# One body for each extra item in nested conditionals, and the item table ahead of the first weight splits

## The chip, the core and the metric

The kernel runs on one core of one Trainium2 chip. The metric is the device time of one execution in microseconds (us); a kernel is timed in several runs and the median counts. Five engines work side by side, each through its own queue: TensorE (PE in the profile, with its weight loads as PEld), VectorE (DVE), ScalarE (ACT), GpSimd (POOL), and SyncE (SP), which only issues transfers. A name with a q behind it (PEldq, SPq, DVEq) is the sequencer of that engine, which reads the instructions, evaluates branches and passes the work on.

## The reference, cut to what matters

```python
attn_out = _attn_ref(q, k, v)                # 8 x 8 heads, 576 rows of 64; keys and values pooled by 8
x = attn_out.transpose(0, 2, 1, 3).reshape(4608, 512)
# experts: 8 of them, each token goes to the one with the largest logit
expert_idx = np.argmax(logits, axis=1)
for e in range(8):
    mask = expert_idx == e
    h = np.maximum(x[mask] @ w1[e], 0.0)     # 512 -> 1024
    out[mask] = gate_w[mask, None] * (h @ w2[e])   # 1024 -> 512
# feed forward
h = out @ w_in                               # 512 -> 2048
return ((h * np.cos(h)) @ w_out)             # 2048 -> 512
```

All arrays are float32. How many tokens go to an expert is only known when the kernel has computed the logits.

## The kernel before

The kernel has three stages: attention with routing (to about 220 us of the profile), the experts (to about 762 us), and the feed-forward part (to the end). The instructions of an engine stand in its queue in the order in which the code issues them; nothing is reordered.

**Items.** Attention writes each token's row to a buffer `xv` in memory, sorted by expert, through indirect transfers that GpSimd issues (`scatter`). `tables` then computes on VectorE, from the number of tokens of each expert, a table with one row for each *item*: an item is up to 128 tokens of one expert. `tab` holds the row of `xv`, the half of the weight buffer and the expert of each item, `cumi` the running number of items, `crow` the output row. There are at least 36 items (`NTILE`, 4608/128) and at most 43 (`NI`); with this input 41 are computed. The first 36 are a plain loop. How many more there are is read from `cumi` into a register (`more`) on TensorE, VectorE and SyncE.

**One item i.** `gemm1(i)` reads from `tab` which weights to use (two register loads on TensorE), waits until they are there (`sem_ready1`), does 24 matmuls into two banks and VectorE applies the relu into `h`. `load(i+3)` fetches a later item's rows on SyncE's queue, `t_x(i+1)` transposes the next item's rows on TensorE (4 transposes) and VectorE splits them in two float32r parts, `gemm2(i-1)` does the second matrix for the item before (24 matmuls), VectorE scales the result and SyncE stores it (L719 to L724), and `t_h` transposes `h` (8 transposes) and VectorE splits it (4 instructions). So TensorE's order is gemm1(i), t_x(i+1), gemm2(i-1), t_h, gemm1(i+1) and so on.

**Weights.** Every weight matrix is used as a high and a low part. A matrix comes in four chunks of 128x1024 into one of 8 raw buffers; `w_hi` rounds a chunk on ScalarE (L129), `w_lo` subtracts the rounded from the raw one (L137) on GpSimd or VectorE. Chunks 0 to 3 are the first matrix of expert 0, chunks 4 to 7 the first matrix of expert 1, 8 to 11 the second matrix of expert 0, 12 to 15 the second of expert 1. With the last chunk of a matrix `sem_ready1` or `sem_ready2` is raised, on which gemm1 or gemm2 waits. The raw buffers of chunks 0 to 7 are filled during attention; chunk j + 8 is loaded when chunk j has been split. Later chunks are all split on GpSimd, by `phase_x`.

**The start of the expert stage** (L896 to L912) is issued in this order: `tables` on VectorE; the loads of items 0 to 2 on SyncE; chunks 3, 6, 7 on GpSimd; chunks 0, 1, 2, 4, 5 on VectorE behind the table; the loads of chunks 8 to 14; `t_x(0)`.

**The end of the loop.** `either` is a binary tree of conditionals with a copy of the remaining items in each of its eight leaves (`items(k)` with k = 0 to 7, so 28 bodies). With 41 items the program goes to `items(5)`. ScalarE and GpSimd take no part in the conditionals. After them come the transposes `t_y` of the first output rows for the feed-forward part, `gemm2` of the last item with the gate that was copied to `gl`, and the feed-forward loop.

Of the kernel before, what the change touches and what calls it, by code (L numbers as in the profile page):

```python
# [18 lines left out]
ENGINES = mybir.EngineType.PE, mybir.EngineType.DVE, mybir.EngineType.SP  # L19
# [3 lines left out]
def attention_moe_ffn_kernel(  # L23
# [13 lines left out]
    nc = tc.nc  # L37
# [4 lines left out]
    E = w1.shape[0]  # L42
# [5 lines left out]
    NTILE = NT // 128  # L48
    REG = NT + 128
    XW = DM + 2  # L50
    NI = NTILE + E - 1
# [17 lines left out]
    def bank(i, name):  # L69
        return psp[0].tile([128, 512], F32, tag=f"p{i}", name=name)  # L70
# [26 lines left out]
    cumi = const.tile([128, E], I32, name="cumi")  # L97

    sem_ready1 = tc.alloc_semaphore("w1_ready")
    sem_ready2 = tc.alloc_semaphore("w2_ready")  # L100
    sem_w1 = tc.alloc_semaphore("items_past_w1")
    sem_free = tc.alloc_semaphore("items_done")


    raws = {}
# [29 lines left out]
    def w_lo(j, eng):  # L135
        t, hi, lo = raws.pop(j)
        i = eng.tensor_tensor(lo, t, hi.bitcast(F32), ALU.subtract)  # L137
        if eng is nc.gpsimd:
            tc.add_to_no_dep_group(W_GROUP, i.ins)
        c = order[j][1]  # L140
        if c % 4 == 3:
            nc.gpsimd.engine_nop().then_inc(sem_ready2 if c > 3 else sem_ready1, 1)

    def apart(group, dma):

# [445 lines left out]
    def tables(sm):  # L591
        V = nc.vector
        cnt, m, ends, ge, g2, top = (sm.tile([128, E], F32, name=t) for t in ("cnt", "m", "ends", "ge", "g2", "top"))
        mi = sm.tile([128, E], I32, name="mi")
        ii, of, ei = (sm.tile([128, 1], F32, name=t) for t in ("ii", "of", "ei"))
        V.tensor_tensor(cnt, base, ebase, ALU.subtract)
        V.tensor_scalar(mi, cnt, 127.0, None, op0=ALU.add)
        V.tensor_scalar(mi, mi, 7, None, op0=ALU.logical_shift_right)
        V.tensor_scalar(m, mi, 1.0, None, op0=ALU.max)
        V.tensor_tensor_scan(ends, one8, m, 0.0, op0=ALU.mult, op1=ALU.add)  # L600
        V.tensor_scalar(ii, ends[:, E - 1:E], -1.0, iot, op0=ALU.add, op1=ALU.min)
        V.tensor_scalar(ge, ends, ii, None, op0=ALU.is_le)
        V.tensor_copy(cumi, ends)
        V.tensor_reduce(ei, ge, axis=AX.X, op=ALU.add)
        V.tensor_tensor(g2, ge, m, ALU.mult)
        V.tensor_scalar(tab[:, 2:3], ei, 1.0, None, op0=ALU.add)
        V.tensor_reduce(of, g2, axis=AX.X, op=ALU.add)
        V.tensor_scalar(tab[:, 1:2], tab[:, 2:3], 1, None, op0=ALU.bitwise_and)
        V.tensor_scalar(of, of, ii, -128.0, op0=ALU.subtract, op1=ALU.mult)

        V.tensor_scalar(top, cnt, -128.0, 0.0, op0=ALU.add, op1=ALU.max)
        V.tensor_scalar(g2, idx8[:, 0, :], NEG, ei, op0=ALU.subtract, op1=ALU.is_equal)
        V.tensor_tensor(g2, g2, top, ALU.mult)
        V.tensor_reduce(ii, g2, axis=AX.X, op=ALU.add)
        V.tensor_tensor(of, of, ii, ALU.min)
        V.tensor_scalar(tab[:, 1:2], tab[:, 1:2], float(SLOT), None, op0=ALU.mult)
        V.scalar_tensor_tensor(tab[:, 0:1], ei, float(REG), of, op0=ALU.mult, op1=ALU.add)
        V.tensor_tensor(g2, ge, cnt, ALU.mult)
        V.tensor_reduce(ei, g2, axis=AX.X, op=ALU.add)
        V.tensor_tensor(crow, ei, of, ALU.add)  # L620
# [14 lines left out]
    def experts_and_feed_forward(slot, wes):  # L635
# [26 lines left out]
        def split(p, hi, lo):  # L662
            pv = p.rearrange("p (k n) -> p k n", k=4)
            nc.vector.tensor_copy(hi, pv)
            nc.vector.tensor_tensor(lo, pv, hi.bitcast(F32), ALU.subtract)

        def t_x(i):
            t = X[i][:, 0:DM].rearrange("p (c k) -> p k c", k=KC)
            p = bank(0, "ptx")
            for kk in range(KC):  # L670
                nc.tensor.transpose(p[:, kk * 128:(kk + 1) * 128], t[:, kk, :], ident)
            split(p, *xT)
# [26 lines left out]
        def t_h():  # L699
            hv = h.rearrange("p (c k) -> p k c", k=FC1)  # L700
            for n in range(FC1 // 4):
                p = bank(4 + n, "pth")
                for kk in range(4):
                    nc.tensor.transpose(p[:, kk * 128:(kk + 1) * 128], hv[:, n * 4 + kk, :], ident)
                split(p, *hT[n])
# [20 lines left out]
        def gate(i):  # L726
            return X[i][:, DM:XW]
# [53 lines left out]
        def wc_load(f):  # L781
            if f < FC2:
                wraw[f] = rawp[0].tile([128, QW], F32, tag="raw", name="wst")
                if f < 3:
                    d = nc.scalar.dma_start(wraw[f], wd[:, f])
                    d.then_inc(sem_wc[f], 16)
                    tc.no_tile_sem_insts.add(d.ins.name)
                    tc.add_to_no_dep_group(f"wc_load{f}", d.ins)
                else:
                    nc.sync.dma_start(wraw[f], wd[:, f])  # L790
# [16 lines left out]
        def y_load(g):  # L807
            for r in range(4):
                n = g * 4 + r
                Y[n] = (xp.tile([128, XW], F32, tag="x", name="yb") if g else y0p.tile([128, XW], F32, tag=f"y{r}", name="yb"))[:, 0:DM + 1]  # L810
                nc.sync.dma_start(Y[n], yv[n * 128:(n + 1) * 128, :])

        def t_y(g, r, b):
            if r == 0:
                X2[g] = x2p[g % 2].tile([128, 2, KC, 512], F32R, tag="x2", name="x2")
            n = g * 4 + r
            t, x2 = Y.pop(n), X2[g][:, :, :, r * 128:(r + 1) * 128]
            p = bank(b, "pt2")
            for kk in range(KC):
                nc.tensor.transpose(p[:, kk * 128:(kk + 1) * 128], t[:, 0:DM].rearrange("p (c k) -> p k c", k=KC)[:, kk, :], ident)  # L820
            pv = p.rearrange("p (k n) -> p k n", k=KC)

            def rest():
                nc.vector.tensor_copy(x2[:, 0], pv)
                nc.vector.tensor_tensor(x2[:, 1], pv, x2[:, 0].bitcast(F32), ALU.subtract)
                nc.vector.tensor_copy(POS[:, n:n + 1], t[:, DM:DM + 1])

            return rest
# [65 lines left out]
        for n in range(NTILE - CHUNKS[-1], NTILE):  # L894
            scatter(n)
        tables(const)  # L896
        for i in range(3):
            load(i)
        for j in (3, 6, 7):
            w_lo(j, nc.gpsimd)  # L900
        for j in (0, 1, 2, 4, 5):
            w_lo(j, nc.vector)
        for j in range(NB, 2 * NB - 1):
            if j == NB + 4:
                conv_load(0)
# [7 lines left out]
        prev = None  # L913
        for i in range(NTILE):
            ex = gemm1(i)
            load(i + 3)
            t_x(i + 1)
            if i:
                gemm2(i - 1, prev, gate(i - 1))
            t_h()  # L920
            prev = ex
            if i == 0:
                phase_x(slot, 16, 8 * E)
            conv_to(i - 1)
            if i == NTILE - 3:
                ces.close()
                y0p = pool("y0p", 1, bes)
            if i == NTILE - 2:
                y_load(0)

        X[NTILE + 3] = xp.tile([128, XW], F32, tag="x", name="xb")
        for i in range(NTILE + 4, NI):
            X[i] = X[i - 5]
        gl, gl2 = (const.tile([128, 2], F32, name=t) for t in ("gl", "gl2"))
        more = nc.values_load(cumi[0:1, E - 1:E], engines=ENGINES, min_val=NTILE, max_val=NI)

        def items(k):
            ex = prev
            for i in range(NTILE, NTILE + k):
                new = gemm1(i)  # L940
                if i + 3 < NTILE + k:
                    load(i + 3)
                if i + 1 < NTILE + k:
                    t_x(i + 1)
                gemm2(i - 1, ex, gate(i - 1))
                t_h()
                ex = new
            nc.vector.tensor_copy(gl, gate(NTILE + k - 1))

        def either(k0, k1):  # L950
            if k1 - k0 == 1:
                items(k0)
                return
            with tc.If(more < NTILE + (k0 + k1) // 2) as cmp:
                either(k0, (k0 + k1) // 2)
            with cmp.Else():
                either((k0 + k1) // 2, k1)

        either(0, E)
        wes.close()  # L960
        x2p = [pool("x2a", 1, side="right")]
        cp = pool("cp", 2, side="right")
        cn = pool("cn", 1, side="right")
        for f in range(3):
            wc_load(f)

        nc.scalar.activation(gl2, gl, AF.Copy)
        for f in range(3):
            wc_split(f, False, W_GROUP)
        for fn in [t_y(0, r, r) for r in range(4)]:  # L970
            fn()
        gemm2(NI, expert(NI), gl)
        bes.close()
        x2p.append(pool("x2b", 1))
# [3 lines left out]
        for n in range(NS + 2):  # L978
# [5 lines left out]
            rest = None  # L984
            if n < NS:
                g, f = seq[n]
                ff1(n)
                if g + 1 < NG:
                    if f == 3:
                        y_load(g + 1)  # L990
                    if f in (6, 8, 10, 12):
                        rest = t_y(g + 1, (f - 6) // 2, 7)
# [21 lines left out]
NB = 8  # L1014
# [41 lines left out]
```

## Time and profile before

| | us |
|---|---|
| median of 3 runs | 1590.6 |
| lowest, highest | 1588.93, 1591.7 |
| the profiled execution | 1594.11 |
| its span, first to last instruction | 1592.4 |
| TensorE busy | 1514.1 (95%) |
| VectorE busy | 1067.1 (67%) |
| ScalarE busy | 413.8 (26%) |
| GpSimd busy | 348.3 (22%) |
| mean granted TensorE clock | 0.987 |

The span is what the trace covers; the execution's own time is 1.7 us longer. Busy time counts the instructions of an engine; a branch, a register load or a wait is not in it. A granted clock of 1.0 is 2.4 GHz and 0.5 is 1.2 GHz.

### The profile page before, as it was taken

Reading aid. Unit: us, or ns where it says so; the run is one execution under the profiler, and the core shown is the slowest. Engines: PE = TensorE matmul, PEld = TensorE weight load, DVE = VectorE, ACT = ScalarE, POOL = GpSimd, SP = SyncE. Lnnn points to the kernel's source line nnn. Section 1 sums busy time; section 2 is a strip of 40 time slices with the busy share of each in tenths; the row PEclk is TensorE's granted clock in tenths of the full one; section 3 lists DMA queues with packets and bytes.
Section 4 is the critical chain, followed back from the end, with each engine's and each line's share of the span. In section 5 each row is a group of like instructions: output and inputs, shape, how many; then the busy total and the mean of one; then the engine's idle time right before and its main releaser. Section 6 shows DMA issues by size and latency. Waiting matters only on the chain.

```text
span 1592.4 us, 22377 instructions
## 1 busy us (share of the span) xinstructions
PE 1514.1 (95%) x7700; PEld 1262.0 (79%) x7700; DVE 1067.1 (67%) x1914; ACT 413.8 (26%) x681; POOL 348.3 (22%) x308
## 2 busy tenths in 40 slices
PE   5999939999999999989999999999999999999997
PEld 4888838887888888868778888888888888888885
DVE  4577776888888888835887556656565655656553
ACT  4677633034000000000433222222222222222221
POOL 6456568089000013000442000010101001010100
PEclk9999969999999999989999999999999999999999
DMA  9853358389433334310322001010101001010000
GB/s 325 254 176 130 126 189 303 118 275 326 131 100 106 118 119 143 93 43 28 114 79 67 0 12 42 7 47 8 47 1 47 7 8 47 7 47 0 28 0 27
DMA packets 66947, 149.05 MB, mean 94 GB/s; under 512 B 10248, under 2 KB 26632, under 8 KB 66832
## 3 DMA queue, kind: packets, MB, share of 16 engines
q1 hardware_dynamic: 52272, 97.10, 19.3%
q10 hardware_dynamic: 8800, 31.48, 6.0%
q0 software_dynamic: 5760, 18.92, 3.1%
q8 instruction: 75, 1.23, 0.3%
q14 instruction: 40, 0.33, 0.1%
HBM read 107.29 MB, written 40.17 MB: 93 GB/s over the span
## 4 chain that ended last, share of the span: by engine, by line
issue 38%; PE 12%; POOL 2%; DVE 0%; ACT 0%; POOLq 0%; ACTq 0%
PE ph L839 6%; PE po L865 5%; POOL out_dram L876 2%; PE pt L820 0%; PE py L715 0%; DVE gl L855 0%; DVE gh L854 0%; ACT L852 0%; POOLq L875 0%; DVE u L853 0%; ACT u L849 0%; ACT u L852 0%; ACT o L873 0%; POOLq L876 0%; POOLq L1051 0%
## 5 line engine op out<-in xcount | busy, mean ns | idle before, releaser
L839 PE MATMUL ph<-x,slot 128*128 128x512 f32 x1728 | 426.6, 396 | 0.0
L839 PEld LDWEIGHTS ph<-x,slot 128*128 128x128 f32 x1728 | 324.5, 188 | 77.0
L865 PE MATMUL po<-slot,gh 128*128 128x512 f32 x1152 | 382.4, 393 | 0.0
L865 PEld LDWEIGHTS po<-slot,gh 128*128 128x128 f32 x1152 | 216.8, 188 | 47.2
L865 PE MATMUL po<-slot,gl 128*128 128x512 f32 x576 | 226.1, 393 | 0.9 <-DVE gl L855 0.9
L137 POOL TENSOR_TENSOR slot<-raw,slot 128x1024 fp32r<-128x1024 f32 x59 | 139.8, 2403 | 258.9 <-ACT slot L129 258.7
L692 PE MATMUL ph<-slot,xh 128*128 (+1 forms) x656 | 178.3, 404 | 17.4 <-issue 7.5
L876 POOL DMA_INDIRECT out_dram<-o,POS x36 | 37.8, 1049 | 694.3 <-ACT o L873 686.1
L849 ACT ACTIVATE u<-ph,quarter 128x512 f32<-128x512 f32 x144 | 98.9, 686 | 348.8 <-PE ph L839 347.9
L850 DVE TENSOR_SCALAR nr<-u 128x512 f32<-128x512 f32 x144 | 62.2, 432 | 164.4 <-ACT u L849 164.4
L853 DVE TENSOR_TENSOR u<-u,ph 128x512 f32<-128x512 f32 x144 | 99.1, 688 | 100.6 <-ACT u L852 100.6
L692 PEld LDWEIGHTS ph<-slot,xh 128*128 128x128 f32 x656 | 121.9, 191 | 44.8 <-issue 7.7
L129 ACT ACTIVATE slot<-raw 128x1024 fp32r<-128x1024 f32 x64 | 66.5, 1060 | 332.6 <-DVEq L696 241.6
L852 ACT ACTIVATE u<-u 128x512 f32<-128x512 f32 x144 | 91.0, 632 | 219.3 <-DVE u L851 217.8
L865 PEld LDWEIGHTS po<-slot,gl 128*128 128x128 f32 x576 | 108.3, 188 | 24.7 <-DVE gl L855 2.2
L855 DVE TENSOR_TENSOR gl<-u,gh 128x512 fp32r<-128x512 f32 x144 | 112.3, 780 | 4.9
L851 DVE TENSOR_TENSOR u<-u,nr 128x512 f32<-128x512 f32 x144 | 99.8, 693 | 5.0
L715 PE MATMUL py<-slot,h0h 128*128 (+1 forms) x328 | 92.0, 402 | 0.0
L692 PE MATMUL ph<-slot,xl 128*128 (+1 forms) x328 | 91.2, 400 | 0.0
L715 PE MATMUL py<-slot,h1h 128*128 (+1 forms) x328 | 88.1, 390 | 0.0
L854 DVE CAST gh<-u 128x512 fp32r<-128x512 f32 x144 | 76.0, 528 | 14.5 <-DVE u L853 0.5
L800 POOL TENSOR_TENSOR slot<-wst,slot 128x512 fp32r<-128x512 f32 x32 | 43.0, 1367 | 192.1 <-ACT slot L796 192.1
(170 smaller groups left out, 1863.4 us busy)
## 6 DMA issues: line engine op xcount, KB each, us to landing
raw<-in_moe_w_dram ACTq DMA_DIRECT2D x57, 512.0 KB, 5.8
xb<-xv SPq DMA_DIRECT2D x41, 257.0 KB, 3.2
yv<-y SPq DMA_DIRECT2D x41, 256.5 KB, 3.2
yb<-yv SPq DMA_DIRECT2D x36, 256.5 KB, 3.6
kraw<-in_k_dram SPq DMA_DIRECT2D x12, 768.0 KB, 8.6
vraw<-in_v_dram SPq DMA_DIRECT2D x12, 768.0 KB, 9.9
q<-in_q_dram SPq DMA_DIRECT2D x8, 1024.0 KB, 10.2
craw<-in_moe_w_in_dram SPq DMA_DIRECT2D x16, 512.0 KB, 4.5
```

The costliest lines, as they stand in the source:

```text
L137: i = eng.tensor_tensor(lo, t, hi.bitcast(F32), ALU.subtract)
L692: mm = nc.tensor.matmul(p, a[:, kk, :], at(so, o + kk * F1 + n * 512), start=(c == 0), stop=(c == 3 * KC - 1))
L715: mm = nc.tensor.matmul(p, a[:, kk, :], at(so, o + W2O + (n * 4 + kk) * DM), start=(c == 0), stop=(c == 3 * FC1 - 1))
L839: nc.tensor.matmul(p, win[:, f, s, kk * 128:(kk + 1) * 128], x2[:, m, kk, :], start=(c == 0), stop=(c == 3 * KC - 1))
L849: nc.scalar.activation(u, p, AF.Identity, scale=1.0 / TWO_PI_EXACT, bias=quarter)
L851: nc.vector.tensor_tensor(u, u, nr, ALU.subtract)
L852: nc.scalar.activation(u, u, AF.Sin, scale=TWO_PI)
L853: nc.vector.tensor_tensor(u, u, p, ALU.mult)
L854: nc.vector.tensor_copy(gh, u)
L855: nc.vector.tensor_tensor(gl, u, gh.bitcast(F32), ALU.subtract)
L865: nc.tensor.matmul(O[g][r], a[:, r * 128:(r + 1) * 128], wout[:, f, s, :], start=(f == 0 and c == 0), stop=(f == FC2 - 1 and c == 2))
L876: apart("out_rows", nc.gpsimd.indirect_dma_start(out=out, out_offset=bass.IndirectOffsetOnAxis(ap=POS[:, g * 4 + r:g * 4 + r + 1], axis=0) ...
```

## The change

The binary tree of conditionals goes; in its place stands a chain of seven conditionals, each nested in the one before, with one body each. The register `more` is read two items earlier. `t_h` of the 36th item leaves the loop and becomes the first step of the first conditional; each body begins with the `t_h` of the item before it, and one `t_h` follows behind the whole chain. A body prepares the next item whether there is one or not (`load`, `t_x`). The gate of the last item is copied to `gl` ahead of the chain and again in each body.

At the start of the expert stage VectorE takes chunks 0 to 3 and GpSimd chunks 4 to 7. VectorE raises a new semaphore `sem_tab` when it is through with the table and its four chunks, and GpSimd waits for that before its first chunk. `sem_ready1` for expert 0 is raised by VectorE. The transposes `t_y` are issued ahead of the splits `wc_split` (other engines).

```diff
-            nc.gpsimd.engine_nop().then_inc(sem_ready2 if c > 3 else sem_ready1, 1)
+            (nc.gpsimd.engine_nop() if eng is nc.gpsimd else eng.drain()).then_inc(sem_ready2 if c > 3 else sem_ready1, 1)
...
         tables(const)
+        for j in range(4):
+            w_lo(j, nc.vector)
+
+        nc.vector.drain().then_inc(sem_tab, 1)
+        nc.gpsimd.wait_ge(sem_tab, 1)
         for i in range(3):
             load(i)
-        for j in (3, 6, 7):
+        for j in range(4, NB):
             w_lo(j, nc.gpsimd)
-        for j in (0, 1, 2, 4, 5):
-            w_lo(j, nc.vector)
...
-            t_h()
+            if i < NTILE - 1:
+                t_h()
...
             if i == NTILE - 2:
                 y_load(0)
+                more = nc.values_load(cumi[0:1, E - 1:E], engines=ENGINES, min_val=NTILE, max_val=NI)
...
-        more = nc.values_load(cumi[0:1, E - 1:E], engines=ENGINES, min_val=NTILE, max_val=NI)
-
-        def items(k):
-            ex = prev
-            for i in range(NTILE, NTILE + k):
+
+        def rest(i, ex):
+
+
+            with tc.If(more > i):
+                t_h()
                 new = gemm1(i)
-                if i + 3 < NTILE + k:
+                if i + 3 < NI:
                     load(i + 3)
-                if i + 1 < NTILE + k:
+                if i + 1 < NI:
                     t_x(i + 1)
                 gemm2(i - 1, ex, gate(i - 1))
-                t_h()
-                ex = new
-            nc.vector.tensor_copy(gl, gate(NTILE + k - 1))
-
-        def either(k0, k1):
-            if k1 - k0 == 1:
-                items(k0)
-                return
-            with tc.If(more < NTILE + (k0 + k1) // 2) as cmp:
-                either(k0, (k0 + k1) // 2)
-            with cmp.Else():
-                either((k0 + k1) // 2, k1)
-
-        either(0, E)
+                nc.vector.tensor_copy(gl, gate(i))
+                if i + 1 < NI:
+                    rest(i + 1, new)
+
+        nc.vector.tensor_copy(gl, gate(NTILE - 1))
+        rest(NTILE, prev)
+        t_h()
...
+        for fn in [t_y(0, r, r) for r in range(4)]:
+            fn()
 
         nc.scalar.activation(gl2, gl, AF.Copy)
         for f in range(3):
             wc_split(f, False, W_GROUP)
-        for fn in [t_y(0, r, r) for r in range(4)]:
-            fn()
         gemm2(NI, expert(NI), gl)
```

## Rows read from the trace of the kernel before

**Rows 1.** The page's first line.

```profile
span 1592.4 us, 22377 instructions
```

**Rows 2.** Waits of PE: engine, line, waited for: total us, times, longest.

```profile
PE ph L692 <- issue: 7.5, 1, 7.5
PE ph L692 <- DVE xh L664: 7.0, 1, 7.0
PE ph L692 <- POOLq L142: 2.3, 1, 2.3
```

**Rows 3.** Timeline, start of the expert stage: start, us, engine, line, operation, count [idle before].

```profile
219.12 0.16 DVE L614 TENSOR_REDUCE ii<-g 128x1 f32<-128x8 f32 x1
219.32 7.31 DVE L615 TENSOR_TENSOR of<-of,ii 128x1 f32<-128x1 f32 x1
219.64 6.96 POOL L137 TENSOR_TENSOR slot<-raw,slot 128x1024 fp32r<-128x1024 f32 x3
...
225.82 1.10 PE L671 MATMUL ptx<-ident,xb 128*128 128x128 f32 x4 [12.65 <-DMA xb<-xv]
...
227.50 5.77 DVE L137 TENSOR_TENSOR slot<-raw,slot 128x1024 fp32r<-128x1024 f32 x5 [0.21 <-issue]
...
233.19 0.68 DVE L664 CAST xh<-ptx 128x512 fp32r<-128x512 f32 x1
...
233.93 2.08 PE L692 MATMUL ph<-slot,xh 128*128 128x512 f32 x4 [7.00 <-DVE xh L664]
...
236.15 9.44 POOL L137 TENSOR_TENSOR slot<-raw,slot 128x1024 fp32r<-128x1024 f32 x4 [9.54 <-ACT slot L129]
...
249.94 1.17 PE L715 MATMUL py<-slot,h0h 128*128 128x512 f32 x4
```

**Rows 4.** Timeline, PE's transposes of t_h around the first conditional.

```profile
681.28 1.06 PE L704 MATMUL pth<-ident,h 128*128 128x128 f32 x8
...
703.68 1.06 PE L704 MATMUL pth<-ident,h 128*128 128x128 f32 x8
...
716.14 1.06 PE L704 MATMUL pth<-ident,h 128*128 128x128 f32 x8
```

**Rows 5.** Windows: stretch, its us, busy us by engine, granted clock (PEclk), DMA.

```profile
689.80:693.40 3.60, 3.55 (x8) 2.81 (x9) 0.00 (x0) 0.00 (x0) 0.00 (x0) 0.50 0.00 0
```

**Rows 6.** Branches (L954) by sequencer, three stretches: ns min/median/max, first and last start.

```profile
L954 PEldq COMPARE_BRANCH  x1: 3478/3478/3478, 679.4 to 679.4; - x1
...
L954 PEldq COMPARE_BRANCH  x2: 78/2578/5078, 683.0 to 683.1; - x2
...
L954 PEldq COMPARE_BRANCH  x1: 3678/3678/3678, 750.7 to 750.7; - x1
...
L954 SPq COMPARE_BRANCH  x4: 38/45/58, 683.5 to 754.7; - x4
```

**Rows 7.** Timeline, end of the last item before the feed-forward part.

```profile
741.01 1.06 PE L704 MATMUL pth<-ident,h 128*128 128x128 f32 x8
...
752.02 1.08 PE L715 MATMUL py<-slot,h1h 128*128 x4
...
752.94 1.06 PE L704 MATMUL pth<-ident,h 128*128 128x128 f32 x8
753.14 0.75 DVE L719 TENSOR_SCALAR y<-py,xb 128x512 f32<-128x512 f32 x1 [4.76 <-PE py L715]
754.01 0.15 DVE L721 COPY y<-xb 128x1 f32<-128x1 f32 x1
754.08 0.68 DVE L664 CAST h0h<-pth 128x512 fp32r<-128x512 f32 x1
...
754.74 2.17 PE L820 MATMUL pt<-ident,yb 128*128 128x128 f32 x16 [0.75 <-SPq L954]
...
761.66 0.69 DVE L825 TENSOR_TENSOR x<-pt,x 128x512 fp32r<-128x512 f32 x1
...
762.39 8.56 PE L839 MATMUL ph<-x,slot 128*128 128x512 f32 x36
```

More of the change, by code (lines that the diff above doesn't have):

```diff
@@ L102, in attention_moe_ffn_kernel @@
     sem_free = tc.alloc_semaphore("items_done")
+    sem_tab = tc.alloc_semaphore("tables")
     raws = {}
```

## The prediction

> **What bounds the kernel now.** I began with the page's first line and busy shares: the span is 1592.4 us [rows 1] and TensorE is busy for 95% of it, so what counts is the time in which TensorE stands still, or runs at the lower clock. The waits of PE name where that is in the expert stage: 7.0 us at the first gemm1, behind VectorE's split of the first item's rows; 7.5 us at a gemm1 for "issue", that is, for nothing that another engine does; and 2.3 us for GpSimd's weights [rows 2]. The last one follows on buffers that TensorE itself frees, so it moves along with TensorE and I leave it. The other two are the two places that the change touches, so I read a timeline of each.
>
> At the first place, the 128x1 table step L615 takes 7.31 us, while its neighbour L614 takes 0.16. In the same time GpSimd does its three chunks (6.96 us from 219.64), and L615 ends when the third does [rows 3]. So the table stands still while GpSimd has the memory that both read; it costs 7.15 us. VectorE's five chunks follow (5.77 us), then the split xh of item 0, at 233.19, though its transposes were done at 225.82 + 1.10 = 226.92. TensorE starts gemm1(0) at 233.93 [rows 3].
>
> At the second place TensorE's t_h of the 36th item starts at 681.28 and the next one at 703.68, 22.40 us later; the one after that follows at 716.14, 12.46 us later [rows 4]. So the first conditional costs 22.40 - 12.46 = 9.94 us. TensorE's sequencer shows of what: a branch of 3.48 us at 679.4, one of 0.08 us, and one of 5.08 us at 683.1 [rows 6]. With 41 items the first and third condition are false (the program jumps over many bodies) and the second true (it goes on with the next instruction): a far jump costs TensorE 3.5 to 5.1 us, going on costs 0.08. After the standstill the clock is at 0.50, its lower level, for the first 3.6 us [rows 5], which is part of the 9.94. SyncE's branches, over far less code, took 0.04 to 0.06 us [rows 6].
>
> **The table and the splits.** GpSimd now waits for the table, so L615 should take its neighbour's 0.16 us and the table end 7.15 us sooner: VectorE's splits begin at 227.50 - 7.15 = 220.35. Four take 4 x 5.77/5 = 4.62 us, to 224.97; the two drains I put at 0.2 us together, as they wait for work that has ended, so GpSimd starts at about 225.2. The rows of item 0 don't move: their load waits for the last scatter, so the transposes still end at 226.92. They are now what sets the start: xh at 226.97 for 0.68 us, gemm1(0) at about 227.7, 6.2 us sooner than 233.93 [rows 3].
>
> Behind GpSimd's wait stand chunks 4 to 7 and then all of phase_x, so I follow its queue: 9.44 us for four chunks [rows 3], so chunk 7 at 225.2 + 9.4 = 234.6 and chunk 11 at 244.1 (before: 236.15 + 9.44 = 245.6). gemm1(1) needs chunk 7 and would start at about 237.7, so it isn't held. gemm2(0) needs chunk 11 and would start at 249.94 - 6.2 = 243.7; it waits until about 244.2. So the front gives 249.94 - 244.2 = **5.7 us**. Its bounds: 6.2 if GpSimd is in time; 4.2 if chunk 11 comes no sooner than before (245.6 and 0.1 for the semaphore). From there TensorE works without a break, and the gain goes through to the end.
>
> The Trainium skill ("SBUF — State Buffer", section "Who interferes with whom") has a VectorE instruction with two SBUF inputs blocked by a GpSimd instruction that reads SBUF, for the whole of that instruction. For one instruction that is 2.3 us, and the front would then give only about 0.9; the row shows the wait over all three, and I go by the row.
>
> **The chain of conditionals.** At the 36th item the condition is true and TensorE goes on with the next instruction; the 9.94 us fall away and the clock stays up. Five true conditions cost 5 x 0.08 = 0.4 us of the sequencer's time, and the earlier read of `more` about as much. The cover is the sequencer's lead: the branch at 750.7 was reached 3.3 us before the transposes ahead of it ended (752.94 + 1.06 = 754.00) [rows 6, 7]. I count these at nothing; without cover it is 0.4. So **9.9 us**, at least 9.5.
>
> **The end of the chain.** Three things are added. First, a t_x for an item 42 that doesn't exist: the last item took 752.94 - 741.01 = 11.93 us without it, others 12.46 [rows 4, 7], so 0.5 us. The two loads too many are on SyncE's queue between stores, with a whole item of slack; nothing. Second, the sixth condition is false and TensorE jumps over two bodies. I take 3.68 us as for the jump at 750.7; with the lead of 3.3 us some 0.4 us show. Third, the last t_h stands behind the join, and it needs VectorE, whose path through the conditionals isn't known when the waits are written, so I expect it to wait for VectorE's last instruction in the chain. Call the end of the last gemm2 in a body T (before: 752.02 + 1.08 = 753.10). VectorE then does L719 (0.75) and L721 (0.15), which ended at 754.16, and the gl copy, so t_h can start at T + 1.3 or so, where it used to follow at once [rows 7]. After 0.6 us of transposes VectorE splits h from T + 1.9; before it started at 754.08, T + 0.98. VectorE was as late as TensorE at the start of the feed-forward part (its last split ends at 761.66 + 0.69 = 762.35, the first matmul starts at 762.39 [rows 7]), so the delay of 0.9 us shows in full. Together **+1.4 us**. Bounds: +0.5 (the transposes of t_h are released at T and the jump hidden) and +4 (the jump takes 5.08 us, and the join waits for a transfer too). The moved lines of t_y and wc_split are on different engines and change no queue.
>
> The sum: -5.7 - 9.9 + 1.4 = -14.2 us. The profiled execution took 1594.1 us, so 1579.9 for a profiled one; it was 3.5 us above the median of the runs, 1590.6, so I predict **1576.4 us**.
>
> **The rivals.** *GpSimd becomes the bound at the front.* Its wait also holds the raw buffers of chunks 12 to 14, and ScalarE's loads queue behind them. For it: gemm2(0) has half a microsecond too little already. Against: chunks 8 to 11 are loaded sooner than before, as VectorE frees their buffers sooner. The front then gives 4.2 or a little less: 1578. *The join costs more:* the +4 above, 1579. For it: at the join before, TensorE did wait 0.75 us for SyncE's L954 [rows 7]. *Going on isn't free:* a true condition shows for 0.5 to 1 us at each of five items, 1579 to 1581. Against: the row of 0.08 us.
>
> *On the other side: every taken jump of TensorE costs a fetch, however short.* Where a conditional has something to make up on its other side, each of five bodies ends with a jump over it. At 3.68 us each that is 18 us, which nothing hides as they follow each other: 1576.4 + 18 = 1595, slower. It decides from 14.2/5 = 2.8 us a jump. For it: all three taken jumps of TensorE took 3.5 us or more. Against: all three were far, and SyncE's took 0.06 us at most [rows 6]. The Trainium skill ("Runtime: NRT & Kernel Launch", section "Instruction fetch mechanics") has a fetch only where the target lies outside the two blocks held; by that rule these jumps are free and the forecast stands, and the far jumps of 3.5 us and more agree with it.
>
> *The change doesn't do what it says:* the table stalls on something else than GpSimd's chunks, and the front gives nothing: 1582.
>
> **How the numbers follow.** Chances: the forecast within its own 1574 to 1578, 0.58; GpSimd at the front 0.12; the join 0.12; going on 0.05; the front without effect 0.04; short jumps dear 0.05; 0.04 for a better result than 1574, if the lower clock at gemm1(0) ends sooner. A measurement of this kernel tells about 0.2% from no change, 3.2 us. Only the short jumps end outside of faster: 1595 is slower, and a jump of 3 us or less is the same. So 0.93 faster, 0.03 same, 0.04 slower. The range from 1573.5 to 1581 leaves out the last, part of the front without effect, and little on the low side.
>
> **What would show it.** Right: L615 at about 0.2 us; gemm1(0) at about 227.7 in the timeline; GpSimd's first chunk near 225; t_h to t_h of 12.46 us throughout items 36 to 40; five branches of TensorE's sequencer near 0.08 us and one of 3.5 us or more; a standstill near 1.3 us ahead of the last t_h. Wrong: several branches of 3.5 us, a wait of PE for POOL of more than 1 us at gemm2(0), or a wait for SyncE at the join of more than 2 us.

## The result and the profile after

The changed kernel took 1575.58 us (median of 4 runs, 1574.05 to 1578.47) beside 1589.78 us for the kernel before (4 runs): a ratio of 0.990 with a 95% interval of 0.9882 to 0.9918, that is 13.0 to 18.8 us less; the medians differ by 14.2. Predicted were 1576.4 us, 14.2 less.

The page of the profiled execution begins so:

```profile
span 1575.3 us, 22422 instructions
```

That is 17.1 us below the span of before [rows 1], more than the medians differ. 2.3 us of it lie ahead of everything that was changed: the last step of the table before the disputed one starts at 216.82, not at 219.12 [rows 3], after attention with the same instructions. In the twelve profiles of this study that step starts anywhere between 214.9 and 221.0 us. So each stretch is measured from its own start below.

The timeline of the changed kernel's front, with the lines that answer to [rows 3] (numbers of lines are one higher):

```profile
216.82 0.16 DVE L615 TENSOR_REDUCE ii<-g 128x1 f32<-128x8 f32 x1
217.02 0.16 DVE L616 TENSOR_TENSOR of<-of,ii 128x1 f32<-128x1 f32 x1
...
218.05 4.63 DVE L138 TENSOR_TENSOR slot<-raw,slot 128x1024 fp32r<-128x1024 f32 x4 [0.21 <-issue]
...
222.96 28.23 POOL L138 TENSOR_TENSOR slot<-raw,slot 128x1024 fp32r<-128x1024 f32 x12 [5.51 <-DVEq L901]
223.26 1.10 PE L672 MATMUL ptx<-ident,xb 128*128 128x128 f32 x4 [12.24 <-DMA xb<-xv]
...
224.46 0.69 DVE L665 CAST xh<-ptx 128x512 fp32r<-128x512 f32 x1 [1.78 <-PE ptx L672]
...
225.21 2.07 PE L693 MATMUL ph<-slot,xh 128*128 128x512 f32 x4 [0.84 <-DVE xh L665]
...
241.90 1.17 PE L716 MATMUL py<-slot,h0h 128*128 128x512 f32 x4 [0.38 <-DVE h L696]
```

The table step takes 0.16 us, VectorE's four chunks begin behind the table, GpSimd begins when they are done, and VectorE then waits 1.78 us for the transposes, whose result used to wait for it. gemm2(0) starts 25.1 us after the start of the step L615; before it was 249.94 - 219.12 = 30.8.

TensorE's t_h around the first and the last conditional, and the first matmuls of the feed-forward part, answer to [rows 4, 7]:

```profile
673.00 1.06 PE L705 MATMUL pth<-ident,h 128*128 128x128 f32 x8
...
697.90 1.06 PE L705 MATMUL pth<-ident,h 128*128 128x128 f32 x8
...
722.78 1.06 PE L705 MATMUL pth<-ident,h 128*128 128x128 f32 x8
...
734.32 1.07 PE L716 MATMUL py<-slot,h1h 128*128 x4
...
735.43 0.75 DVE L720 TENSOR_SCALAR y<-py,xb 128x512 f32<-128x512 f32 x1 [3.73 <-PE py L716]
736.29 0.15 DVE L722 COPY y<-xb 128x1 f32<-128x1 f32 x1
736.37 0.16 DVE L953 COPY gl<-xb 128x2 f32<-128x2 f32 x1
...
736.74 1.13 PE L705 MATMUL pth<-ident,h 128*128 128x128 f32 x8 [1.36 <-DVEq L945]
...
737.71 2.09 PE L821 MATMUL pt<-ident,yb 128*128 128x128 f32 x16
...
745.11 8.62 PE L840 MATMUL ph<-x,slot 128*128 128x512 f32 x36
```

From 673.00 to 697.90 two items pass in 24.90 us, 12.45 each, where the first alone took 22.40. The last t_h waits 1.36 us for the sequencer of VectorE at the join (L945). The branches of TensorE's sequencer, in two stretches (ahead of 725 us, and after):

```profile
L945 PEldq COMPARE_BRANCH  x5: 72/73/85, 668.9 to 718.7; - x5
...
L945 PEldq COMPARE_BRANCH  x2: 193/1890/3587, 731.1 to 735.7; - x2
...
L945 PEldq EVENT_SEMAPHORE  x2: 51/51/51, 735.4 to 735.6; - x2
```

Five true conditions at 0.07 to 0.09 us each; one false one, 3.59 us; one jump at the join (the place behind the whole chain), 0.19 us.

### The profile page after: what moved, and what is told of

It is laid out like the page before. It is cut to its first block, busy times and chain, and to the rows that moved or that the text cites. A ratio compares the mean times of both kernels' runs of the same rounds, so it can differ in the third digit from the quotient of the medians.

```text
span 1575.3 us, 22422 instructions
## 1 busy us (share of the span) xinstructions
PE 1512.9 (96%) x7704; PEld 1261.1 (80%) x7704; DVE 1060.5 (67%) x1920; ACT 413.7 (26%) x681; POOL 348.6 (22%) x309
## 4 chain that ended last, share of the span: by engine, by line
issue 39%; PE 11%; POOL 2%; DVE 1%; DMA 0%; ACT 0%; POOLq 0%; DVEq 0%; SPq 0%
PE ph L840 5%; PE po L866 5%; POOL out_dram L877 2%; DMA wst<-wd 0%; PE pt L821 0%; DVE x L825 0%; DVE gl L856 0%; DVE gh L855 0%; DVE x L826 0%; DVE nr L851 0%; POOLq L876 0%; DVE u L852 0%; DVE h0h L665 0%; PE pth L705 0%; DVE u L854 0%
```

## The experiments

All stretches in one table, worked out from the starts in each timeline (us). "Front" is from the table step ahead of the disputed one (L614 before, L615 after) to gemm2(0); "first" from the t_h of the 36th item to the next; "rest" from there to the last t_h; "end" from the last t_h to the first matmul of the feed-forward part. The last column is the ratio to the kernel before, timed on the same chip, with its interval.

| kernel | front | first | rest | end | ratio |
|---|---|---|---|---|---|
| before | 30.8 | 22.4 | 49.3 | 9.45 | |
| changed | 25.1 | 12.4 | 51.3 | 8.37 | 0.9900 (0.9882 to 0.9918) |
| changed, again | 25.2 | 12.4 | 51.3 | 8.37 | 0.9900 (0.9884 to 0.9916) |
| front alone | 25.1 | 22.6 | 49.3 | 9.47 | 0.9957 (0.9943 to 0.9970) |
| chain alone | 30.9 | 12.4 | 51.3 | 8.37 | 0.9956 (0.9938 to 0.9973) |
| GpSimd without the wait | 33.7 | 12.4 | 51.3 | 8.37 | 0.9972 (0.9962 to 0.9983) |
| wait for the table alone | 33.1 | 12.4 | 51.3 | 8.37 | 0.9939 (0.9921 to 0.9957) |
| tree turned round | 31.4 | 15.6 | 49.3 | 9.38 | 0.9967 (0.9954 to 0.9980) |
| t_h ahead, five chunks | 24.7 | 12.4 | 49.8 | 13.10 | 0.9914 (0.9891 to 0.9937) |
| five chunks | 25.1 | 12.4 | 51.3 | 8.37 | 0.9910 (0.9897 to 0.9924) |

From the first matmul of the feed-forward part all of them take 830.0 to 830.1 us to the end. The items between gemm2(0) and the 36th t_h took 431.1 to 433.1 us in these kernels, where their code is the same.

### Each half alone

The front of the change on the tree of before (the new semaphore and the line that raises `sem_ready1` are as in the change):

```diff
...
+        for j in range(4):
+            w_lo(j, nc.vector)
+
+        nc.vector.drain().then_inc(sem_tab, 1)
+        nc.gpsimd.wait_ge(sem_tab, 1)
         for i in range(3):
             load(i)
-        for j in (3, 6, 7):
+        for j in range(4, NB):
             w_lo(j, nc.gpsimd)
-        for j in (0, 1, 2, 4, 5):
-            w_lo(j, nc.vector)
```

> The kernel before with the change of the front alone: table, four chunks on VectorE, then GpSimd; the tree of conditionals stays. Theory (the table step stood still for GpSimd's chunks, and the gain goes through to the end): the table step takes 0.2 us, gemm2(0) comes 5.7 us sooner, the first conditional keeps its 22.4 us from t_h to t_h, and the kernel is 5 to 6.2 us faster than before. Rival (the front's gain is given back later in the expert stage, at a wait for weights): within 1 us of before, with a longer wait of PE for GpSimd in the loop.

The chain of the change behind the front of before (the same diff, undone in the changed kernel):

> The changed kernel with the front of before: only the chain of conditionals. Theory: from t_h to t_h 12.5 us at every item past the 36th instead of 22.4 at the first, about 1 us given back at the end of the chain, so 8.5 to 9.5 us faster than before; the table step still takes 7.3 us. Rival (the two parts are worth something only together): less than 5 us.

The front alone gives 30.8 - 25.1 = 5.7 us in its stretch, the chain alone 22.4 - 12.4 = 10.0 at the first conditional and gives back 2.0 - 1.1 = 0.9 (unrounded 0.96) behind it. The timings say 6.8 us (4.8 to 9.1) and 7.0 us (4.3 to 9.9) less; the second is below the 9.0 of the stretches, inside its interval. In both kernels each stretch is that of the parent it comes from, to 0.2 us. So the parts add up, and neither needs the other.

### What holds the table step

GpSimd's wait moved from ahead of its chunks to behind them, so that it holds up nothing but the semaphore for expert 1:

```diff
         if c % 4 == 3:
+            if j == 7:
+                nc.gpsimd.wait_ge(sem_tab, 1)
...
         nc.vector.drain().then_inc(sem_tab, 1)
-        nc.gpsimd.wait_ge(sem_tab, 1)
```

> The changed kernel, but GpSimd doesn't wait ahead of its chunks 4 to 7 (it waits for VectorE only ahead of raising the semaphore for expert 1, behind them). Theory (GpSimd's chunks keep the table step from the memory that both read): the step takes as long as GpSimd's four chunks, 9 to 10 us, and gemm1(0) starts some 8 us later than in the changed kernel; 7 to 8.5 us slower than the changed kernel. Rival (the front gains by sharing the chunks four and four, and the wait does nothing): the step takes 0.2 us and the time is that of the changed kernel.

The timeline of this kernel at the step (L618 here):

```profile
218.07 9.71 DVE L618 TENSOR_TENSOR of<-of,ii 128x1 f32<-128x1 f32 x1
...
218.52 9.23 POOL L138 TENSOR_TENSOR slot<-raw,slot 128x1024 fp32r<-128x1024 f32 x4
```

With four chunks on GpSimd the step takes 9.71 us and ends when the fourth does; with three it was 7.31 [rows 3]. The front takes 33.7 us, 8.6 more than in the changed kernel and 2.9 more than before. Sharing the chunks four and four is therefore worth nothing without the wait; the rival falls. In the timings this kernel is still 4.5 us faster than before (2.7 to 6.0), all of it from the chain.

Then the wait for the table alone, with GpSimd's chunks beside VectorE's:

```diff
         if c % 4 == 3:
+            if j == 7:
+                nc.gpsimd.wait_ge(sem_tab, 2)
...
         tables(const)
+        nc.vector.drain().then_inc(sem_tab, 1)
         for j in range(4):
             w_lo(j, nc.vector)
```

(The raise behind VectorE's chunks stays and is now the second; GpSimd waits for it ahead of the semaphore for expert 1.)

> The changed kernel, but GpSimd waits for the table alone and starts its chunks together with VectorE's four. Theory (VectorE's subtractions read two operands from SBUF as the table step did, and GpSimd, once it has the memory, keeps it over all its chunks): the table stays short, and one of two things shows: either GpSimd is first and a VectorE subtraction stands still for 9 us, with gemm1(0) 5 to 8 us later than in the changed kernel, or VectorE is first and GpSimd begins when the last of the four ends, as with the wait. I expect the first, 5 to 8 us slower than the changed kernel. Rival (only the short table steps suffer; the long ones share the memory): chunks side by side at 1.2 and 2.4 us, and the time of the changed kernel or up to 0.5 us less.

Its timeline:

```profile
215.59 0.16 DVE L618 TENSOR_TENSOR of<-of,ii 128x1 f32<-128x1 f32 x1
...
216.60 12.19 POOL L138 TENSOR_TENSOR slot<-raw,slot 128x1024 fp32r<-128x1024 f32 x4 [0.58 <-DVEq L900]
...
216.91 12.96 DVE L138 TENSOR_TENSOR slot<-raw,slot 128x1024 fp32r<-128x1024 f32 x4 [0.50 <-issue]
```

The table step is short, as GpSimd begins only behind it, and the loss comes later: four of VectorE's subtractions alone take 4.63 us and four of GpSimd's 9.44 [rows 3], together 14.1; side by side they need 12.96 and 12.19. They take turns, nearly one at a time; the trace has most of them at 3.1 to 3.4 us each, where alone they take about 1.2 and 2.4. The front takes 33.1 us, 8.0 more than in the changed kernel. The price that I expected is there, but not in the form: no single subtraction stood still for 9 us. So GpSimd must wait for VectorE's chunks too, not for the table alone. The timings put this kernel 9.7 us ahead of before (6.9 to 12.6), where its stretches make 9.0 - 2.3 = 6.7; against the changed kernel's ratio it is some 6 us slower, as expected.

The Trainium skill ("SBUF — State Buffer", section "Who interferes with whom") has the loser blocked for the whole of the other's instruction. The turns of this run agree with that; the 7.31 and 9.71 us of the single small step, over three and four instructions of GpSimd, are more than it says.

### What a conditional costs

The tree of before with its conditions turned round, so that the program falls into the larger half:

```diff
-            with tc.If(more < NTILE + (k0 + k1) // 2) as cmp:
-                either(k0, (k0 + k1) // 2)
-            with cmp.Else():
-                either((k0 + k1) // 2, k1)
+            with tc.If(more > NTILE + (k0 + k1) // 2 - 1) as cmp:
+                either((k0 + k1) // 2, k1)
+            with cmp.Else():
+                either(k0, (k0 + k1) // 2)
```

> The kernel before with the conditions of the tree turned round, so that with 41 items two of the three conditions lead on to the next instruction and only one jumps far (before: two jumped far). The bodies are the same. Theory (each far jump costs TensorE's sequencer 3.5 to 5 us, and its lead of 3.3 us hides about one of them): one branch of 3.5 us or more and two near 0.08, a standstill of 1.5 to 3.5 us instead of 7.5, the clock stays up or nearly, and 5 to 8 us faster than before. Rival (the standstill comes with reading the register and evaluating conditions there, however the program goes on): the standstill stays at 7 us or more, and the time is that of before.

Timeline and branches of this kernel at the first conditional:

```profile
679.39 1.06 PE L704 MATMUL pth<-ident,h 128*128 128x128 f32 x8
...
683.36 1.17 PE L692 MATMUL ph<-slot,xh 128*128 x4 [2.91 <-DVE h1l L665]
...
694.99 1.06 PE L704 MATMUL pth<-ident,h 128*128 128x128 f32 x8
```

```profile
L954 PEldq COMPARE_BRANCH  x3: 77/82/3602, 677.5 to 681.3; - x3
```

One far jump of 3.60 us in place of 3.48 and 5.08, with the same register read and three conditions: the standstill is 2.91 us instead of 7.5, the granted clock behind it is 1.00 (from 683.4 to 687.0 us) where it was 0.50 [rows 5], and the item takes 15.6 us instead of 22.4. So it is the far jumps that cost, and the second one above all, because the sequencer's lead is used up by the first. The lead doesn't make one jump free: the jump ended at 681.28, 0.8 us after the transposes (679.39 + 1.06 = 680.45), and the other 2.1 us went mostly to the register loads for the next item, which the lead hides in the items after it. With one far jump the item is still 15.6 - 12.45 = 3.1 us longer. The timings put this kernel 5.3 us ahead of before (3.2 to 7.3).

Then two false conditionals put behind t_h of the 20th item of the changed kernel, each jumping over transposes that are never done, 8 or 200 of them:

```diff
+        over = nc.values_load(cumi[0:1, E - 1:E], engines=ENGINES, min_val=NTILE, max_val=NI)
         for i in range(NTILE):
...
+            if i == 19:
+                for _ in range(2):
+                    with tc.If(over > NI - 1):
+                        p = bank(7, "skip")
+                        for _ in range(8):
+                            nc.tensor.transpose(p[:, 0:128], ident, ident)
```

> The changed kernel with two false conditionals more, behind t_h of the 20th item; each jumps over 8 transposes that are never done (the code is there, the result is the same). Theory (a false condition costs TensorE much only where the target is far): two branches of 0.2 us or less on TensorE, and less than 1.5 us from t_h to t_h above the usual 12.45. Rival (every taken jump of TensorE costs a fetch): two branches of 3.5 us, the item about 6 to 10 us longer.

> The same two false conditionals, each over 200 transposes that are never done. Theory: two branches of 3.5 us or more in a row; the lead of 3.3 us hides about one, so the item becomes 4 to 10 us longer, and more if the clock drops behind the standstill, as at the first conditional of the kernel before. Rival (the price hangs on the conditional, not on the distance): the same as with 8 transposes.

Timeline and branches with 8 transposes:

```profile
472.57 1.06 PE L705 MATMUL pth<-ident,h 128*128 128x128 f32 x8
475.88 1.19 PE L693 MATMUL ph<-slot,xh 128*128 x4 [2.26 <-DVE h1h L665]
...
489.09 1.06 PE L705 MATMUL pth<-ident,h 128*128 128x128 f32 x8
```

```profile
L929 PEldq COMPARE_BRANCH  x2: 207/225/243, 470.3 to 473.8; - x2
L929 PEldq EVENT_SEMAPHORE  x2: 51/51/51, 473.7 to 474.1; - x2
```

And with 200:

```profile
471.86 1.06 PE L705 MATMUL pth<-ident,h 128*128 128x128 f32 x8
479.23 2.07 PE L693 MATMUL ph<-slot,xh 128*128 x4 [6.30 <-DVE ca L755]
...
492.23 1.06 PE L705 MATMUL pth<-ident,h 128*128 128x128 f32 x8
```

```profile
L929 PEldq COMPARE_BRANCH  x2: 3317/3849/4381, 469.6 to 474.2; - x2
```

The branches are as the theory has them: 0.21 and 0.24 us over 8 transposes, 3.3 and 4.4 us over 200, so the rival that every taken jump costs a fetch falls (each of the two kernels ran once; the reading is from their traces). It agrees with the Trainium skill ("Runtime: NRT & Kernel Launch", section "Instruction fetch mechanics"), by which only a target outside the blocks held is fetched. But the short ones were dearer than expected: the item took 489.09 - 472.57 = 16.5 us, 4.1 more than 12.45, where I had less than 1.5; with the far ones 20.4 us, 7.9 more. The 2.26 us of standstill are not in the branches. TensorE's sequencer stops at the join until TensorE itself is done (its two semaphore events there stand at 473.7 and 474.1 us, and the transposes end at 472.57 + 1.06 = 473.6), and the two register loads for the next item, else hidden by its lead, come behind that (474.2 to 475.7 us). Another 1.6 us pass in the matmuls behind, where the granted clock was 0.64 on the mean from 475.8 to 480.0 us. So a false conditional has a price beside the jump: it takes the sequencer's lead.

The distance alone doesn't set the jump's price either. The false condition at the end of the chain jumps over the same two bodies in every kernel that has the chain; it took 3.33 to 3.73 us in six traces, but 0.85 and 0.65 us in these two kernels and 1.41 us in the next one. In these three the branch stands at another place in TensorE's instructions. Whether that is the reason was not tried. The 8 and 200 transposes shift the code as well, so these two runs show that the price differs with what is jumped over, but not by which rule.

### t_h ahead of the join, and five chunks

```diff
-            if i < NTILE - 1:
-                t_h()
+            t_h()
...
             with tc.If(more > i):
-                t_h()
                 new = gemm1(i)
...
                 gemm2(i - 1, ex, gate(i - 1))
+                t_h()
                 nc.vector.tensor_copy(gl, gate(i))
...
         rest(NTILE, prev)
-        t_h()
...
-        for j in range(4):
+        for j in range(5):
             w_lo(j, nc.vector)
```

(GpSimd then takes chunks 5 to 7.)

> The changed kernel with t_h back ahead of each branch (so at the end of the chain it runs under the far jump and doesn't wait for VectorE's way through the join) and five chunks on VectorE, three on GpSimd (VectorE stands idle for 1.8 us there, and gemm2(0) waits 0.4 us for GpSimd). Theory: the wait of 1.4 us ahead of the last t_h goes and 0.7 us ahead of t_y comes, 0.4 us saved; gemm2(0) doesn't wait, 0.4 us saved; together 0.5 to 1 us less than the changed kernel, which the timing can't tell, but the stretches of the trace can. Rival (the join costs the same wherever t_h stands): no gain at the end.

Timelines of this kernel at the join, of TensorE, of VectorE, and TensorE's branches with VectorE's event at the join:

```profile
735.30 1.06 PE L705 MATMUL pth<-ident,h 128*128 128x128 f32 x8
739.40 3.28 PE L821 MATMUL pt<-ident,yb 128*128 128x128 f32 x16 [3.05 <-DMA yv<-y]
```

```profile
738.48 0.69 DVE L666 TENSOR_TENSOR h1l<-pth,h1h 128x512 fp32r<-128x512 f32 x1
739.09 0.16 DVE L952 COPY gl<-xb 128x2 f32<-128x2 f32 x1
```

```profile
L944 PEldq COMPARE_BRANCH  x7: 65/73/1410, 670.8 to 736.7; - x7
...
L944 DVEq EVENT_SEMAPHORE  x1: 21/21/21, 739.3 to 739.3; - x1
```

My theory of the end fell. t_y, now first behind the join, waits 3.05 us, and from the t_h of the 37th item to the feed-forward part this kernel needs 49.8 + 13.1 = 62.9 us, the changed one 59.7. The profile names a store (yv) as the releaser, but TensorE goes on 0.1 us after VectorE's event at the join, and VectorE comes to that only when it has split h. The trace has TensorE's own waits: the long one (2.18 us, to 739.35) is on VectorE's semaphore, and the one on the store's took 0.05 us. So what stands first behind the join waits for all that VectorE still has in front of it. With t_h behind the join that is only the scaling of the output and two copies. The order of the change is the better one; my rival, no gain, was nearer, but it is a loss of 3.2 us. The front of this kernel took 24.7 us, 0.4 less than the changed one. So the five chunks were run alone, beside the changed kernel once more.

> The changed kernel once more, on the chip of the next one and beside the kernel before. If the sum of the stretches holds (5.7 us at the front, 9.9 at the first conditional, 1 given back at the end), 14 to 15 us faster than before, whatever attention takes in an execution.

> The changed kernel with five chunks on VectorE and three on GpSimd, t_h left where the change put it. Theory: gemm2(0) no longer waits for GpSimd's chunk 11, so it comes 0.4 us sooner counted from the table; the end of the chain keeps its wait of 1.4 us ahead of t_h. 0.4 us less than the changed kernel, too little for the timing to tell. Rival (the fifth chunk holds up VectorE's xh and so gemm1(0), and gemm2(0) with it): gemm2(0) at the same time or later.

The changed kernel came out at 0.990 again, 13.4 to 18.5 us less, and its stretches are the same. The five chunks alone took 25.1 us to gemm2(0), no less than four; TensorE doesn't wait for GpSimd there, but eight matmuls of gemm1(0) that took 2.04 us in the changed kernel took 2.48 in this one, as the granted clock was 0.50 until 233.2 us and 0.76 on the mean from there to 235.2. The second run of the changed kernel shows the same (2.44 us, no wait, 25.2 us), and the kernel with both changes took 2.06 us and 24.7. So how long the lower clock lasts in gemm1(0), which differs between traces, hides what the fifth chunk is worth: some 0.4 us at best. At 0.991 the kernel can't be told from the changed one. No run here beats the change.

## Why the prediction was right, and where it was off

*The table and the splits* (-5.7 us): right to 0.1, with its steps. L616 0.16 us; GpSimd at 222.96 and gemm1(0) at 225.21, which with the 2.3 us of attention are 225.3 and 227.5 where 225.2 and 227.7 were predicted; gemm2(0) waits 0.38 us. The profile puts that wait on VectorE's relu, but TensorE also waits there for GpSimd's chunk 11, which ends at 222.96 + 8 x 28.23/12 = 241.8. In the two kernels with skipped conditionals, whose front does the same work, the profile names GpSimd's semaphore for a wait of 0.5 and 1.0 us at this place; in the second run of the changed kernel there is no wait. That the wait and not the sharing does it is shown by the run without it.

*The chain* (-9.9 us): right; 22.4 to 12.4, five true conditions at 0.07 us that show nowhere, and the clock stays up. That the far jumps were the cause is shown by the tree turned round: one far jump less gives 6.8 of the 10 us. The other 3.1 stood with the jump that was left; what the late read of `more` adds to them was not tried apart.

*The end of the chain* (+1.4 us): measured +1.0 (0.96), and the parts are not those of the sum. The prediction names three parts, 0.5, 0.4 and 0.9 us, which make 1.8; its 1.4 has no place for the jump's 0.4, and it gives no reason. The t_x too many (+0.5) and t_h's wait for VectorE (1.36 us, predicted 1.3) are right. The far jump shows nowhere: it ended before TensorE's own matmuls did, and the sequencer then waited for these. The step that failed is "the delay of 0.9 us shows in full". It rested on the end of VectorE's last split, 761.66 + 0.69 = 762.35. But the first eight matmuls of the feed-forward part need only the high halves of the splits (L824 before, L825 after). In the kernel before:

```profile
760.95 0.68 DVE L824 CAST x<-pt 128x512 fp32r<-128x512 f32 x1
```

In the changed kernel:

```profile
744.27 0.68 DVE L825 CAST x<-pt 128x512 fp32r<-128x512 f32 x1
744.99 0.69 DVE L826 TENSOR_TENSOR x<-pt,x 128x512 fp32r<-128x512 f32 x1
```

Before, the last high half was there at 761.63, 0.76 us ahead of the first matmul, so VectorE was not as late as it looked in [rows 7]; now it is there at 744.95, 0.16 us ahead, and the last split ends only after that matmul has begun. TensorE's own way got shorter besides: t_y follows t_h at once now, where it used to wait 0.75 us for SyncE. From the end of the last gemm2 in a body to the feed-forward part it is 9.72 us (745.11 - 735.39), against 9.29 before: 0.4 us of the 0.9.

*The rival of the short jumps*: there are not five jumps at the ends of the bodies but one, 0.19 us, and a short jump costs TensorE 0.21 to 0.24 us. Its only ground in the rows were three jumps that were all far. The other rivals fell as well: in the changed kernel gemm2(0) waits 0.38 us at most for GpSimd, no wait for SyncE shows at the join, and the items behind true conditions take 12.45 us.

The time itself was hit closer than its steps warrant, and that is in part luck: the runs of one kernel spread over 3 to 7 us, and attention alone differs by 6 us between profiles. The prediction took 1579.9 us for a profiled execution and 3.5 us off for the median; the profiled one took 1576.99, which is 2.9 less, 2.3 of it in attention, and lay only 1.4 above the median. The stretches add up to 14.7 us, against 14.2 predicted.

## What to carry to other kernels

A short instruction of VectorE with two operands in SBUF stood still here until GpSimd was through with three or four subtractions; let GpSimd wait for the critical table, and for VectorE's long instructions too if the two would only take turns. Lay out conditionals so that the likely way is the one that goes on with the next instruction: TensorE paid 3.3 to 5.3 us for most far jumps here (0.65 to 1.41 in three traces). Its lead of some 3 us hides most of one jump, but then not the register loads behind it: with one far jump the item was 3.1 us longer, with two 7.9 to 10.1, the lower clock behind the standstill included. Behind a conditional that was skipped, put first what needs least of the engine that arrives last.

## What the runs showed of the hardware

One small table step stood still over several instructions of GpSimd in a row (7.31 us over three, 9.71 over four), while long subtractions of VectorE took turns with them (12.96 us for four beside 12.19). By the recorded starts the small step was first both times, by 0.32 and 0.45 us. Why it doesn't get its turn was not tried. Two skipped conditionals over 8 transposes made an item 4.1 us longer though their branches took 0.45 us together. The same jump over two bodies took 3.33 to 3.73 us in six traces and 0.65 to 1.41 in three others; why is open.
